# A fused attention and feed-forward block: pacing feed-forward and output matmuls over each query chunk, and filling the free PSUM bank

## The chip, the cores and the metric

The kernel runs on one core of one Trainium2 chip. A core has a matrix engine (PE, TensorE), a vector engine (DVE), an activation engine (ACT), a general engine (POOL), a queue for transfers (SP) and 16 DMA engines. The metric is the device time of one execution in microseconds; the number given for a kernel is the median of several runs.

## The reference

One transformer block on 2048 tokens of width 512, bf16, with attention and feed-forward in parallel, both on the same normalised input:

```
xn  = layernorm(x)                                  # x: 1 x 2048 x 512
qkv = xn @ wqkv                                     # 32 heads of 16
p   = softmax(q @ k.T * 16**-0.5);  A = (p @ v) @ wo
B   = (silu(xn @ w1) * (xn @ w3)) @ w2              # hidden width 1792
out = x + A + B
```

## The kernel before

**Stages.** The head loads x, normalises it, and transposes it into `xnT` (512 x 2048, four blocks of 128 rows). Then attention runs over units: four query chunks of 512 tokens (`NQC`), in each eight groups of four heads (`NG`), in each two halves of 256 queries (the very last half is cut into two of 128). There are 65 units.

Each unit goes through the scores twice. Pass one (`p1`, L755) computes scores with queries on the partitions; each step is two matmuls of 512 keys into a pair of PSUM banks (0 and 1, or 2 and 3), and DVE takes the row maximum of the 128 x 1024 result (L774). 16 steps make a unit of 256 queries, 1024 the whole kernel (`NP1`), 256 a query chunk. The negated maxima are written into spare rows of the query operand, so that pass two (`p2`, L869), which computes the scores again with keys on the partitions, has the maximum already subtracted; ACT takes the exponential out of banks 4 to 6 into one of 44 slots of `PT` (L885, 2048 of them, two for each maximum). The third step, PV, multiplies the exponentials by V (`Vaug`, with a column of ones for the sum of the row) in 16 groups, in bank 7; ACT copies the result out (L949), and two DMAs, a power and a product on POOL normalise it into `onorm`.

Bank 7 is shared, one tenant at a time, by all work that is tiled over columns: the projections QT, KT and V, PV, and the two parts that the change is about. Feed-forward (`ffn_pair`, 14 pairs `G`, `U` for each query chunk, each of four groups of four 512-column matmuls) ends with three ACT evacuations (tanh L627, gate L629, up L633) and three products on POOL into `hT`. The output (`OUT`, four tiles of 128 tokens for each chunk, each one group for x, 14 for `hT` and `w2`, 8 for `onorm` and `wo`) is evacuated by ACT (L688) and stored. For the last chunk the output is in two parts: `OUTA` (x and `hT`, 15 groups a tile, in bank 7, kept in SBUF) and `OUTB` (`onorm`, 8 groups a tile, in banks 0 to 3 once all maxima are taken), added by DVE (L713).

All column-tiled groups are issued by one helper (`col_groups`), so that their matmuls stand under one line, L447. Such a group is four matmuls at once, each into another quarter of the columns of the PE array. `p1` and `p2` are tiled over rows instead: each matmul uses 32 of the 128 rows.

**What sets the order.** The program's order is fixed when it is built. A planner keeps a model of each engine's time with fixed costs (`_c_mm`, `_c_act`, `_c_dve`), and step by step lets the engine go on whose next item could start first. `assign` gives bank 7 to the tile that `choose` names: projections that are due soon, then a PV that is ready, then `outs`, then `ffn` in its order. `pred_g` says when a feed-forward pair may start: its weights have landed, the pair two before it is done, and the output tiles of the chunk before are done (they read `hT`). So before the change the feed-forward of a chunk starts as soon as it may, and runs as fast as bank 7 and its evacuations go. `pick_pe` then decides between a `p1` step (a), a `p2` step (b) and the next column group (c): c goes when it ends before a could start, else a goes, and a b that could start earlier than a goes first.

Semaphores follow from recorded reads and writes. A column group that takes bank 7 waits for the ACT evacuation of the tenant before; PE issues in order, so what is queued behind it waits too.

Of the kernel before, what the change touches and what calls it, by code (L numbers as in the profile page):

```python
# [197 lines left out]


class _Tile:  # L200
    __slots__ = ("groups", "evac", "name", "bank", "pred", "need", "on_start")

    def __init__(self, name, groups, evac, pred=None, need=None, on_start=None):
        self.name = name
        self.groups = groups
        self.evac = evac
        self.pred = pred
        self.need = need
        self.on_start = on_start
        self.bank = None  # L210
# [10 lines left out]
def _c_mm(n):  # L221
    return n / 2400.0 + 0.006


def _build(nc, A_x, A_wqkv, A_wo, B_w1, B_w3, B_w2, out):
    S, D = A_x.shape[1], A_x.shape[2]
    H = D // 16
    NG = H // 4
    DC = D // 128
    F = B_w1.shape[1]  # L230
    FC = F // 128
    NT = S // 128
    NQC = S // 512
# [6 lines left out]
    TOL = 0.15  # L240
    STARVE = 0.7
    COUP = 0.1

    units = []
    for qc in range(NQC):
# [14 lines left out]
    with ctx:  # L260
# [337 lines left out]
            return _Tile("QT2_%d" % u, groups, evac, need=-1)  # L598


        def ffn_pair(sc, fc):
            idx = sc * FC + fc
            sl = idx % 3
            ss = idx % 2
            cnt = [0]

            def part_done(op):
                cnt[0] += 1
                if cnt[0] < 3:
                    return  # L610
                q = poolq["ffn"]
                q.append(_Item(lambda e: e.tensor_scalar(t1[:, :], th[:, ss, :], 1.0, 1.0, ALU.mult, ALU.add),  # L612
                               [("th", ss)], [("t1",)], 0.62, 0.72))
# [12 lines left out]
            def evac_g(bk):  # L626
                return [_Item(lambda e: e.activation(th[:, ss, :], bank(bk), ACTF.Tanh, scale=0.5),  # L627
                              [("ps", bk)], [("th", ss)], _c_act(512), cb=part_done),
                        _Item(lambda e: e.activation(zg[:, ss, :], bank(bk), ACTF.Identity, scale=0.5),  # L629
                              [("ps", bk)], [("zg", ss)], _c_act(512), cb=part_done)]  # L630

            def evac_u(bk):
                return [_Item(lambda e: e.activation(ub[:, ss, :], bank(bk), ACTF.Identity),  # L633
                              [("ps", bk)], [("ub", ss)], _c_act(512), cb=part_done)]

            def pred_g():
                if ("w13", idx) not in done:
                    return False
                if idx >= 2 and ("hT", idx - 2) not in done:
                    return False  # L640
                if sc == 0:
# [6 lines left out]
            return [_Tile("G%d_%d" % (sc, fc), groups(0), evac_g, pred=pred_g, on_start=start_g),  # L648
                    _Tile("U%d_%d" % (sc, fc), groups(1), evac_u)]


        def load_xr(tg):
# [24 lines left out]
        def tile_OUT(tg):  # L677
            qc, ts = divmod(tg, 4)
            groups = [g_x(tg)] + [g_h(ts, fc) for fc in range(FC)]
            groups += [g_on(qc, ts, g, False, g == NG - 1) for g in range(NG)]  # L680

            def evac(bk):
                def cb(op):
                    store(tg)
                    done.add(("OUT", tg))
                    if tg + 4 < NT:
                        load_xr(tg + 4)
                return [_Item(lambda e: e.activation(osb[:, tg % 4, :], bank(bk), ACTF.Identity),  # L688
                              [("ps", bk)], [("osb", tg % 4)], _c_act(512), cb=cb)]
            return _Tile("OUT%d" % tg, groups, evac, pred=lambda: ("xr", tg) in done  # L690
                         and (tg < 4 or ("ST", tg - 4) in done)
                         and all(("hT", qc * FC + fc) in done for fc in range(FC))
                         and all(("ON", qc, g, ts) in done for g in range(NG)))

        def tile_OUTA(tg):
            qc, ts = divmod(tg, 4)
# [28 lines left out]
            p1 += p1_list(u)  # L725
        NP1 = len(p1)
        p1_n = [0]
        red_n = [0]
        pend_fin = []

        def p1_cand():
# [19 lines left out]
            def emit():  # L751
                def f(e):
                    for i in range(2):
                        j = 2 * pair + i
                        ins = e.matmul(bank(2 * sl + i), QT[32 * j:32 * j + 32, qs, q * 128:(q + 1) * 128],  # L755
                                       KT[32 * j:32 * j + 32, g, kc * 512:(kc + 1) * 512],
                                       start=True, stop=True, tile_position=(32 * j, 0))
                    return ins
                P.pe(f, reads, writes, "row", rows, _c_mm(512), name="p1_%d" % n, first="dve")
                p1_n[0] += 1  # L760
                par = u % 2
# [12 lines left out]
                redq.append(_Item(lambda e: e.tensor_reduce(  # L774
                    part[:, par, qt, 2 * pair:2 * pair + 2, kc],
                    ps[:, sl * 1024:(sl + 1) * 1024].rearrange("p (a b) -> p a b", b=512), AX.X, ALU.max),
                    writes, [("part", par, qt, pair, kc)], _c_dve(1024), cb=cb))
# [56 lines left out]
        def p2_cand():  # L834
# [28 lines left out]
            def emit():  # L863
# [3 lines left out]
                def f(e):  # L867
# [4 lines left out]
                                       start=True, stop=True, tile_position=(32 * j, 0))  # L872
                    return ins
                P.pe(f, reads, writes, "row", (j,), kpb * _c_mm(nq), name="p2_%d" % n, first="act")
                p2_n[0] += 1
                pt_slot[(u, kb, j)] = sl
                if not rest:
# [209 lines left out]
        def col_cand():  # L1087
            best = None
            for t in active:
                if not t.groups:  # L1090
                    continue
                g = t.groups[0]
                if g[3] is not None and not g[3]():
                    continue
                reads = g[1]() if callable(g[1]) else g[1]
# [8 lines left out]
            def emit():  # L1104
                g = t.groups.pop(0)
                P.pe(g[0](t.bank), reads, writes, "col", None, dur, name=t.name)
                if len(g) > 4:
                    g[4]()
                if not t.groups:
# [15 lines left out]
            return st, emit, dur  # L1125

        couple = [-1.0]

        def pick_pe():
            a = p1_cand()  # L1130
            b = p2_cand()
            c = col_cand()
            now = P.free["pe"]
            end = max(now, max(P.rg))

# [110 lines left out]
        assert not (expq or miscq or redq or dveq or spq or active or crit or outs or ffn or tail_outs), "stuck"  # L1246
        assert p1_n[0] == NP1 and p2_u[0] == NU and pv_u[0] == NU and all(("ST", t) in done for t in range(NT))

        P.check()
        sems = {e: ctx.enter_context(nc.semaphore("c_" + e)) for e in _ENGS if e != "sp"}  # L1250
        dma_sems = [ctx.enter_context(nc.semaphore("d%d" % i)) for i in range(_NDMA_SEMS)]
# [62 lines left out]
```

## Time and profile before

| | |
|---|---|
| median of 3 runs | 1380.99 us (1380.11 to 1382.21) |
| span of the profiled execution | 1371.5 us |
| PE busy | 1228.5 us (90%) |
| DVE busy | 1215.0 us (89%), of it the row maxima (L774) 1190.2 |
| ACT busy | 1227.7 us (90%), of it the exps (L885) 1095.5 |
| POOL busy | 357.4 us (26%) |
| first and last row maximum start | 19.7 and 1293.6 us |
| first and last exp start | 62.7 and 1364.8 us |

The profile is one execution as the hardware profiler took it; the span is from its first to its last instruction. "Busy" is the time in which an engine has at least one instruction under way; a matmul that is streaming slowly counts as busy as one that is streaming fast. PEclk, beside it, is the share of the full TensorE clock that was granted. A row of a table by stage has the stretch, its length, the busy time with the number of instructions in brackets, then the granted clock, the DMA share and GB/s. A row of the waits has who waited, for whom, the total in us, how often, and the longest.

### The profile page before, as it was taken

How to read it: one execution, taken by the hardware profiler on the slowest of the kernel's cores; microseconds unless marked ns; L12 is line 12 of the kernel's file. 1: busy time of each engine (PE TensorE's matmuls, PEld its weight loads, DVE VectorE, ACT ScalarE, POOL GpSimd, SP SyncE). 2: the span in 40 equal slices, each digit the busy share in tenths (PEclk: the TensorE clock that was granted, in tenths of full speed). 3: DMA queues.
4: the chain of work that ended last, by engine and by line, in shares of the span. 5: the costliest groups of instructions: out<-in, count | busy, mean ns of one | idle time of the engine just before them, and what ended most of it. 6: DMA issues, size and time to landing. Idle time of an engine off the chain costs nothing.

```text
span 1371.5 us, 36041 instructions
## 1 busy us (share of the span) xinstructions
PE 1228.5 (90%) x15257; PEld 435.0 (32%) x15257; DVE 1215.0 (89%) x1141; ACT 1227.7 (90%) x2413; POOL 357.4 (26%) x453
## 2 busy tenths in 40 slices
PE   5988888899999888899999888899999988899998
PEld 2323322333332332333333322333333333233324
DVE  6898999998898999998899999989989999899702
ACT  5698999998898999988899999989989999899864
POOL 4033332211111245411111244421111144431100
PEclk9998999886578999976679999966669999899555
DMA  8011111000000112100000111100001111100000
GB/s 215 5 31 27 25 24 24 18 10 7 9 18 23 40 32 45 33 10 10 8 14 21 39 39 41 39 9 8 10 6 26 33 41 31 38 9 11 5 3 18
DMA packets 112834, 36.07 MB, mean 26 GB/s; under 512 B 98232, under 2 KB 112672, under 8 KB 112672
## 3 DMA queue, kind: packets, MB, share of 16 engines
q1 hardware_dynamic: 112672, 33.76, 11.6%
q8 instruction: 120, 1.97, 0.6%
q14 instruction: 42, 0.34, 0.1%
HBM read 22.81 MB, written 2.10 MB: 18 GB/s over the span
## 4 chain that ended last, share of the span: by engine, by line
PE 58%; ACT 38%; issue 2%; DMA 1%; DVE 0%; SPq 0%; POOL 0%
ACT PT L885 28%; PE ps L447 27%; PE ps L869 20%; PE ps L755 10%; ACT th L627 2%; ACT ub L633 2%; ACT zg L629 2%; ACT QT L573 1%; ACT U L949 1%; ACT KT L530 1%; DMA hT<-in_A_wqkv_dram 1%; ACT osb L688 0%; ACT osb L485 0%; DVE R L938 0%; SPq L380 0%
## 5 line engine op out<-in xcount | busy, mean ns | idle before, releaser
L774 DVE TENSOR_REDUCE part<-ps 128x2 f32<-128x1024 f32 x1024 | 1190.2, 1219 | 83.5 <-PE ps L869 49.1
L885 ACT ACTIVATE PT<-ps 128x512 bf16<-128x512 f32 x2048 | 1095.5, 641 | 109.0 <-PE ps L869 96.6
L869 PE MATMUL ps<-QT,KT 32*128 32x256 bf16 (+1 forms) x4160 | 676.2, 308 | 39.3 <-ACT PT L885 23.8
L755 PE MATMUL ps<-KT,QT 32*128 32x512 bf16 x2048 | 517.9, 434 | 4.3 <-DVE part L774 4.2
L869 PEld LDWEIGHTS ps<-QT,KT 32*128 32x128 bf16 x4160 | 197.9, 96 | 395.0 <-ACT PT L885 314.3
L447 PE MATMUL ps<-PT,Vaug 128*17 128x256 bf16 (+1 forms) x4160 | 214.2, 323 | 14.9 <-ACT ub L633 5.0
L972 POOL TENSOR_TENSOR Rc<-Lc,mone 128x8 f32<-128x8 f32 x62 | 101.4, 1636 | 398.0 <-DMA Lc<-U 397.9
L447 PE MATMUL ps<-xnT,w 128*32 128x512 bf16 x1792 | 144.9, 394 | 45.8 <-ACT zg L629 19.9
L755 PEld LDWEIGHTS ps<-KT,QT 32*128 32x128 bf16 x2048 | 126.0, 95 | 149.3 <-issue 89.8
L447 PEld LDWEIGHTS ps<-PT,Vaug 128*17 128x17 bf16 x4160 | 91.2, 99 | 132.5 <-issue 84.1
L614 POOL TENSOR_TENSOR a<-zg,ub 128x512 f32<-128x512 bf16 x56 | 64.7, 1155 | 128.8 <-ACT ub L633 128.8
L447 PEld LDWEIGHTS ps<-xnT,w 128*32 128x32 bf16 x1792 | 38.5, 95 | 115.8 <-issue 99.8
L616 POOL TENSOR_TENSOR hT<-a,t 128x512 bf16<-128x512 f32 x56 | 71.0, 1268 | 3.2
L791 POOL TENSOR_SCALAR Z<-negm 128x8 bf16<-128x8 f32 x64 | 14.6, 228 | 210.0 <-DVE negm L815 210.0
L447 PE MATMUL ps<-w,hT 128*32 128x512 bf16 x896 | 67.0, 395 | 0.0
L938 DVE RECIPROCAL R<-ps 128x128 f32<-128x128 f32 (+1 forms) x3 | 3.7, 1224 | 63.7 <-PE ps L447 63.7
L994 POOL TENSOR_TENSOR on_b<-U,R 128x256 bf16<-128x256 f32 x32 | 23.2, 725 | 105.8 <-DMA R<-Rrow 105.8
L447 PE MATMUL ps<-xnT,wq 128*32 128x512 bf16 (+2 forms) x576 | 43.4, 388 | 7.8 <-ACT U L949 2.1
L447 PE MATMUL ps<-xnT,wk_on 128*32 128x512 bf16 x512 | 41.7, 402 | 7.9 <-ACT KT L530 4.8
L994 POOL TENSOR_TENSOR wk_on<-U,R 128x256 bf16<-128x256 f32 x30 | 21.8, 727 | 89.3 <-DMA R<-Rrow 89.3
L612 POOL TENSOR_SCALAR t<-th 128x512 f32<-128x512 bf16 x56 | 34.7, 619 | 24.9 <-ACT th L627 22.8
L633 ACT ACTIVATE ub<-ps 128x512 bf16<-128x512 f32 x56 | 34.8, 622 | 1.2 <-PE ps L447 1.2
(73 smaller groups left out, 408.8 us busy)
## 6 DMA issues: line engine op xcount, KB each, us to landing
w<-in_B_w_dram SPq DMA_DIRECT2D x112, 128.0 KB
R<-Rrow SPq DMA_DIRECT2D x248, 16.0 KB
PT<-in_A_x_dram SPq DMA_DIRECT2D x4, 512.0 KB
xr<-in_A_x_dram SPq DMA_DIRECT2D x16, 128.0 KB
out_dram<-osb SPq DMA_DIRECT2D x16, 128.0 KB
QT<-Zs SPq DMA_DIRECT2D x122, 2.0 KB
w<-in_B_w_dram SPq DMA_DIRECT2D x1, 1792.0 KB
hT<-in_A_wqkv_dram SPq DMA_DIRECT2D x3, 512.0 KB
```

Of the source, the lines that this page charges most:

```text
L447: ins = e.matmul(bank(bk)[32 * i:32 * i + m, c0:c0 + ncols], make_lhsT(i), rhs_ap(i), start=start, stop=stop, tile_position=(0, 32 * i), **kw)
L612: q.append(_Item(lambda e: e.tensor_scalar(t1[:, :], th[:, ss, :], 1.0, 1.0, ALU.mult, ALU.add), [("th", ss)], [("t1",)], 0.62, 0.72))
L614: q.append(_Item(lambda e: e.tensor_tensor(a32[:, :], zg[:, ss, :], ub[:, ss, :], ALU.mult), [("zg", ss), ("ub", ss)], [("a32",)], 1.1, 1.25))
L616: q.append(_Item(lambda e: e.tensor_tensor(hT[:, fc, :], a32[:, :], t1[:, :], ALU.mult), [("a32",), ("t1",)], [("hT", fc)], 1.25, 1.35, cb ...
L627: return [_Item(lambda e: e.activation(th[:, ss, :], bank(bk), ACTF.Tanh, scale=0.5), [("ps", bk)], [("th", ss)], _c_act(512), cb=part_don ...
L633: return [_Item(lambda e: e.activation(ub[:, ss, :], bank(bk), ACTF.Identity), [("ps", bk)], [("ub", ss)], _c_act(512), cb=part_done)]
L755: ins = e.matmul(bank(2 * sl + i), QT[32 * j:32 * j + 32, qs, q * 128:(q + 1) * 128], KT[32 * j:32 * j + 32, g, kc * 512:(kc + 1) * 512], ...
L774: redq.append(_Item(lambda e: e.tensor_reduce(part[:, par, qt, 2 * pair:2 * pair + 2, kc], ps[:, sl * 1024:(sl + 1) * 1024].rearrange("p ( ...
L869: ins = e.matmul(bank(b)[:, i * nq:(i + 1) * nq], KT[32 * j:32 * j + 32, g, (k0 + i) * 128:(k0 + i + 1) * 128], QT[32 * j:32 * j + 32, qs, ...
L885: expq.append(_Item(lambda e: e.activation(PT[:, sl, :], bank(b), ACTF.Exp, scale=SCALE), [("ps", b)], [("PT", sl)], _c_act(512), cb=cb))
L972: poolq["nrm"].append(_Item(lambda e: e.tensor_tensor(Rc[:, pp, 0:nl], Lc[:, pp, 0:nl], mone[:, 0:nl], ALU.pow), [("Lc", pp), ("mone",)], ...
L994: poolq["nrm"].append(_Item(lambda e: e.tensor_tensor(onorm[ob][:, g, q0:q0 + nq], U[:, us, 0:nq], R[:, pp, 0:nq], ALU.mult), [("U", us)] ...
```

## The change

There are two edits, both in the planner; no engine gets another kind of instruction.

*Pacing.* The counter `p1_n` of issued `p1` steps serves as a clock. A feed-forward pair `fc` of chunk `sc` may not start before `ffn_from(sc, fc)`: the 14 starts are spread evenly from count 40 to 300 in chunk 0, from 100 after the chunk's start to 44 after its end in chunks 1 and 2, and from 868 to 1000 in the last. Besides, each group of a `G`, `U` or `OUT` tile needs a positive balance of tokens: a `p1` step adds 3000 (up to 4096 in all), a group takes 2048, the columns that its four matmuls stream. `OUTA`, `OUTB`, PV and the projections are not paced. After the last `p1` step no group is.

*Filling.* Each matmul step is logged with the time at which the planner starts it and with its columns (1024 for `p1`, 512 for `p2`, 1024 for a PV group, 2048 for another column group). When there is no column group to issue, bank 7 has no tenant, `p1_n` is at least 64 and under 1024, and the log of the last 3.0 us holds fewer than 11200 columns, a spare group goes into bank 7: four matmuls of 512 columns with `ident` as weights and `xnT` as data. Nothing reads what it writes.

```
--- before.py
+++ after.py
@@ -198,10 +198,11 @@
 
 
 class _Tile:
-    __slots__ = ("groups", "evac", "name", "bank", "pred", "need", "on_start")
-
-    def __init__(self, name, groups, evac, pred=None, need=None, on_start=None):
+    __slots__ = ("groups", "evac", "name", "bank", "pred", "need", "on_start", "paced")
+
+    def __init__(self, name, groups, evac, pred=None, need=None, on_start=None, paced=False):
         self.name = name
+        self.paced = paced
         self.groups = groups
         self.evac = evac
         self.pred = pred
@@ -240,6 +241,11 @@
     TOL = 0.15
     STARVE = 0.7
     COUP = 0.1
+    PACE = 3000
+    PACE_CAP = 4096
+    LAG = 44
+    LOAD_WIN = 3.0
+    LOAD_MIN = 11200
 
     units = []
     for qc in range(NQC):
@@ -598,6 +604,14 @@
             return _Tile("QT2_%d" % u, groups, evac, need=-1)
 
 
+        CHUNK = 2 * NG * 16
+
+        def ffn_from(sc, fc):
+            last = sc == NQC - 1
+            lo = sc * CHUNK + (100 if sc else 40)
+            hi = (sc + 1) * CHUNK + (-24 if last else LAG)
+            return lo + (hi - lo) * fc // FC
+
         def ffn_pair(sc, fc):
             idx = sc * FC + fc
             sl = idx % 3
@@ -638,6 +652,8 @@
                     return False
                 if idx >= 2 and ("hT", idx - 2) not in done:
                     return False
+                if p1_n[0] < ffn_from(sc, fc):
+                    return False
                 if sc == 0:
                     return all(("V", t) in done for t in range(NT)) and not _wk_pending() and not _wq_pending()
                 return all(("OUT", (sc - 1) * 4 + ts) in done for ts in range(4))
@@ -645,8 +661,8 @@
             def start_g():
                 if idx + 2 < NQC * FC:
                     load_w13(idx + 2)
-            return [_Tile("G%d_%d" % (sc, fc), groups(0), evac_g, pred=pred_g, on_start=start_g),
-                    _Tile("U%d_%d" % (sc, fc), groups(1), evac_u)]
+            return [_Tile("G%d_%d" % (sc, fc), groups(0), evac_g, pred=pred_g, on_start=start_g, paced=True),
+                    _Tile("U%d_%d" % (sc, fc), groups(1), evac_u, paced=True)]
 
 
         def load_xr(tg):
@@ -690,7 +706,7 @@
             return _Tile("OUT%d" % tg, groups, evac, pred=lambda: ("xr", tg) in done
                          and (tg < 4 or ("ST", tg - 4) in done)
                          and all(("hT", qc * FC + fc) in done for fc in range(FC))
-                         and all(("ON", qc, g, ts) in done for g in range(NG)))
+                         and all(("ON", qc, g, ts) in done for g in range(NG)), paced=True)
 
         def tile_OUTA(tg):
             qc, ts = divmod(tg, 4)
@@ -725,6 +741,7 @@
             p1 += p1_list(u)
         NP1 = len(p1)
         p1_n = [0]
+        tokens = [0]
         red_n = [0]
         pend_fin = []
 
@@ -758,6 +775,8 @@
                     return ins
                 P.pe(f, reads, writes, "row", rows, _c_mm(512), name="p1_%d" % n, first="dve")
                 p1_n[0] += 1
+                tokens[0] = min(tokens[0] + PACE, PACE_CAP)
+                note_load(st, 1024)
                 par = u % 2
 
                 def cb(op):
@@ -872,6 +891,7 @@
                                        start=True, stop=True, tile_position=(32 * j, 0))
                     return ins
                 P.pe(f, reads, writes, "row", (j,), kpb * _c_mm(nq), name="p2_%d" % n, first="act")
+                note_load(st, 512)
                 p2_n[0] += 1
                 pt_slot[(u, kb, j)] = sl
                 if not rest:
@@ -1092,6 +1112,8 @@
                 g = t.groups[0]
                 if g[3] is not None and not g[3]():
                     continue
+                if t.paced and tokens[0] <= 0 and p1_n[0] < NP1:
+                    continue
                 reads = g[1]() if callable(g[1]) else g[1]
                 writes = [("ps", t.bank)]
                 st = P.pe_start("col", None, P.ready("pe", reads, writes))
@@ -1104,6 +1126,9 @@
             def emit():
                 g = t.groups.pop(0)
                 P.pe(g[0](t.bank), reads, writes, "col", None, dur, name=t.name)
+                if t.paced:
+                    tokens[0] -= 2048
+                note_load(st, 1024 if t.name.startswith("PV") else 2048)
                 if len(g) > 4:
                     g[4]()
                 if not t.groups:
@@ -1125,11 +1150,33 @@
             return st, emit, dur
 
         couple = [-1.0]
+        loadlog = []
+
+        def note_load(st, w):
+            loadlog.append((st, w))
+            while loadlog and loadlog[0][0] < st - LOAD_WIN:
+                loadlog.pop(0)
+
+        def fill_cand():
+            if 7 in bank_tenant or head_tiles or p1_n[0] < 64 or p1_n[0] >= NP1:
+                return None
+            writes = [("ps", 7)]
+            st = P.pe_start("col", None, P.ready("pe", (), writes))
+            if sum(w for t, w in loadlog if t >= st - LOAD_WIN) >= LOAD_MIN:
+                return None
+
+            def emit():
+                P.pe(col_groups(7, lambda i: ident[:, 32 * i:32 * i + 32], lambda i: xnT[:, 0, 0:512], 512),
+                     [("ident",)] + xnT_keys(0, 512), writes, "col", None, _c_mm(512), name="fill")
+                note_load(st, 2048)
+                n_fill[0] += 1
+            return st, emit, _c_mm(512)
+        n_fill = [0]
 
         def pick_pe():
             a = p1_cand()
             b = p2_cand()
-            c = col_cand()
+            c = col_cand() or fill_cand()
             now = P.free["pe"]
             end = max(now, max(P.rg))
 
@@ -1246,6 +1293,7 @@
         assert not (expq or miscq or redq or dveq or spq or active or crit or outs or ffn or tail_outs), "stuck"
         assert p1_n[0] == NP1 and p2_u[0] == NU and pv_u[0] == NU and all(("ST", t) in done for t in range(NT))
 
+        P.n_fill = n_fill[0]
         P.check()
         sems = {e: ctx.enter_context(nc.semaphore("c_" + e)) for e in _ENGS if e != "sp"}
         dma_sems = [ctx.enter_context(nc.semaphore("d%d" % i)) for i in range(_NDMA_SEMS)]
```

More of the change, by code (lines that the diff above doesn't have):

```diff
@@ L200, with __init__ @@
 class _Tile:
-    __slots__ = ("groups", "evac", "name", "bank", "pred", "need", "on_start")
-    def __init__(self, name, groups, evac, pred=None, need=None, on_start=None):
+    __slots__ = ("groups", "evac", "name", "bank", "pred", "need", "on_start", "paced")
+    def __init__(self, name, groups, evac, pred=None, need=None, on_start=None, paced=False):
         self.name = name
+        self.paced = paced
         self.groups = groups
@@ L242, in _build @@
     COUP = 0.1
+    PACE = 3000
+    PACE_CAP = 4096
+    LAG = 44
+    LOAD_WIN = 3.0
+    LOAD_MIN = 11200
     units = []
@@ L598, in tile_QT2, with ffn_from @@
             return _Tile("QT2_%d" % u, groups, evac, need=-1)
+        CHUNK = 2 * NG * 16
+        def ffn_from(sc, fc):
+            last = sc == NQC - 1
+            lo = sc * CHUNK + (100 if sc else 40)
+            hi = (sc + 1) * CHUNK + (-24 if last else LAG)
+            return lo + (hi - lo) * fc // FC
         def ffn_pair(sc, fc):
@@ L640, in pred_g @@
                     return False
+                if p1_n[0] < ffn_from(sc, fc):
+                    return False
                 if sc == 0:
@@ L647, in start_g @@
                     load_w13(idx + 2)
-            return [_Tile("G%d_%d" % (sc, fc), groups(0), evac_g, pred=pred_g, on_start=start_g),
-                    _Tile("U%d_%d" % (sc, fc), groups(1), evac_u)]
+            return [_Tile("G%d_%d" % (sc, fc), groups(0), evac_g, pred=pred_g, on_start=start_g, paced=True),
+                    _Tile("U%d_%d" % (sc, fc), groups(1), evac_u, paced=True)]
         def load_xr(tg):
@@ L692, in tile_OUT @@
                          and all(("hT", qc * FC + fc) in done for fc in range(FC))
-                         and all(("ON", qc, g, ts) in done for g in range(NG)))
+                         and all(("ON", qc, g, ts) in done for g in range(NG)), paced=True)
         def tile_OUTA(tg):
@@ L727, in _build @@
         p1_n = [0]
+        tokens = [0]
         red_n = [0]
@@ L760, in emit @@
                 p1_n[0] += 1
+                tokens[0] = min(tokens[0] + PACE, PACE_CAP)
+                note_load(st, 1024)
                 par = u % 2
@@ L874, in emit @@
                 P.pe(f, reads, writes, "row", (j,), kpb * _c_mm(nq), name="p2_%d" % n, first="act")
+                note_load(st, 512)
                 p2_n[0] += 1
@@ L1094, in col_cand @@
                     continue
+                if t.paced and tokens[0] <= 0 and p1_n[0] < NP1:
+                    continue
                 reads = g[1]() if callable(g[1]) else g[1]
@@ L1106, in emit @@
                 P.pe(g[0](t.bank), reads, writes, "col", None, dur, name=t.name)
+                if t.paced:
+                    tokens[0] -= 2048
+                note_load(st, 1024 if t.name.startswith("PV") else 2048)
                 if len(g) > 4:
@@ L1127, in _build, with note_load, fill_cand, emit @@
         couple = [-1.0]
+        loadlog = []
+        def note_load(st, w):
+            loadlog.append((st, w))
+            while loadlog and loadlog[0][0] < st - LOAD_WIN:
+                loadlog.pop(0)
+        def fill_cand():
+            if 7 in bank_tenant or head_tiles or p1_n[0] < 64 or p1_n[0] >= NP1:
+                return None
+            writes = [("ps", 7)]
+            st = P.pe_start("col", None, P.ready("pe", (), writes))
+            if sum(w for t, w in loadlog if t >= st - LOAD_WIN) >= LOAD_MIN:
+                return None
+            def emit():
+                P.pe(col_groups(7, lambda i: ident[:, 32 * i:32 * i + 32], lambda i: xnT[:, 0, 0:512], 512),
+                     [("ident",)] + xnT_keys(0, 512), writes, "col", None, _c_mm(512), name="fill")
+                note_load(st, 2048)
+                n_fill[0] += 1
+            return st, emit, _c_mm(512)
+        n_fill = [0]
         def pick_pe():
@@ L1131, in pick_pe @@
             b = p2_cand()
-            c = col_cand()
+            c = col_cand() or fill_cand()
             now = P.free["pe"]
@@ L1247, in _build @@
         assert p1_n[0] == NP1 and p2_u[0] == NU and pv_u[0] == NU and all(("ST", t) in done for t in range(NT))
+        P.n_fill = n_fill[0]
         P.check()
```

## The prediction

> **What bounds the kernel now.** I read the page first: the span, the engines' shares, the slices.
>
> ```profile
> span 1371.5 us, 36041 instructions
> PE 1228.5 (90%) x15257; PEld 435.0 (32%) x15257; DVE 1215.0 (89%) x1141; ACT 1227.7 (90%) x2413; POOL 357.4 (26%) x453
> DVE  6898999998898999998899999989989999899702
> PEclk9998999886578999976679999966669999899555
> ```
>
> Three engines stand at about 90%, so none is an obvious bound. The last row tells more: the granted TensorE clock sinks four times, and where it sinks DVE's digit goes from 9 to 8. The medians before are at 1380.99 us and the span is 1371.5, so 9.5 us lie around the span; I add them at the end. With runs from 1380.11 to 1382.21, about 0.2% (2.8 us) is what can be told from no change.
>
> Next the waits, for what DVE (the row maxima, L774) and ACT (the exps, L885) stand still for.
>
> ```profile
> ACT PT L885 <- PE ps L869: 96.6, 183, 2.8
> DVE part L774 <- PE ps L869: 49.1, 91, 1.3
> DVE part L774 <- PE ps L755: 25.2, 31, 4.9
> ```
>
> Both wait for score matmuls on PE, DVE for 74.3 us in all. That is the store from which a faster PE could pay while maxima run.
>
> Then the row maxima (L774) by stage. The columns are from:to, length, DVE busy (count), granted clock, DMA. The last row is from a narrower stretch; an instruction on a border is counted on both sides, so I take one off each count.
>
> ```profile
> 265.00:435.00 170.00, 152.27 (x131) 0.70 0.06 12
> 435.00:590.00 155.00, 151.67 (x132) 0.98 0.17 36
> 590.00:710.00 120.00, 106.08 (x91) 0.67 0.05 8
> 780.00:900.00 120.00, 115.91 (x101) 0.97 0.17 35
> 900.00:1025.00 125.00, 110.74 (x95) 0.63 0.05 9
> 1260.00:1295.00 35.00, 32.36 (x28) 0.69 0.05 7
> 1295.00:1371.50 76.50, 0.00 (x0) 0.54 0.03 10
> 1203.00:1260.00 57.00, 56.26 (x50) 1.00 0.05 9
> ```
>
> The four low-clock stretches (0.63 to 0.70) are 450 us with 345 - 4 = 341 maxima: 1.320 us each. The three full-clock stretches (0.97 to 1.00) are 332 us with 283 - 3 = 280: 1.186 us each. In the latter DVE is busy 97 to 99% of the time, so DVE is the bound there; in the low-clock ones (88 to 92%) PE is. The last 76.5 us have no maximum at all: a tail of exps, second matmuls and output. So the kernel is bound by DVE at full clock, by PE at the low clock, and by PE again in the tail.
>
> What makes the clock sink? I cut the trace at the borders at which it changes, 3.41 us apart. First two steps of all PE work, then the column-tiled matmuls (the helper's L447) of the second of them.
>
> ```profile
> 341.36:344.77 3.41, 3.41 (x22) 0.50 0.13 19
> 395.96:399.37 3.41, 3.41 (x62) 1.00 0.06 7
> 395.96:399.37 3.41, 2.59 (x44) 1.00 0.06 7
> ```
>
> Both steps have PE busy from end to end; one is granted 0.50, the other 1.00. So it is not busy time that decides; the steps differ in how many matmuls stream, 22 against 62. Now one step that is followed by a fall and one that is followed by a rise: for each its L447 matmuls, how many of these are PV (the tile view of PT), its L755, its L869, and the clock of the step after.
>
> ```profile
> 402.79:406.20 3.41, 0.51 (x12) 1.00 0.02 5
> 402.79:406.20 3.41, 1.39 (x6) 1.00 0.02 5
> 402.79:406.20 3.41, 1.92 (x14) 1.00 0.02 5
> 406.20:409.61 3.41, 3.41 (x50) 0.50 0.09 19
> 433.51:436.92 3.41, 2.21 (x20) 0.50 0.04 7
> 433.51:436.92 3.41, 0.00 (x0) 0.50 0.04 7
> 433.51:436.92 3.41, 1.40 (x4) 0.50 0.04 7
> 433.51:436.92 3.41, 1.23 (x10) 0.50 0.04 7
> 436.92:440.33 3.41, 3.41 (x62) 1.00 0.10 15
> ```
>
> (In the first step the tile view gives the same row as L447: all 12 are PV, of 256 columns.) Columns streamed: 12 x 256 + 6 x 512 + 14 x 256 = 9,700, and the clock falls; 20 x 512 + 4 x 512 + 10 x 256 = 14,800, and it rises. The switching point lies between, if columns are the measure. The change's own mark, 11200 in 3.0 us, is 12,700 in 3.41: inside.
>
> The Trainium skill ("TensorE: Matmul & The Clock Gate", "What's actually happening" and "HAM oscillation") has a clock of half or full by windows of about 3.4 us, which the trace shows, and says that PE keeps it as long as no idle gap exceeds about 3.4 us. The trace differs on that: the step at 341.36 was busy for all of its 3.41 us at 0.50. By that rule neither spreading nor fills would matter to the clock.
>
> **The change part by part.** *Spreading.* It removes no matmul of the reference. Columns per maximum follow from the counts of the groups:
>
> ```profile
> L869 PE MATMUL ps<-QT,KT 32*128 32x256 bf16 (+1 forms) x4160 | 676.2, 308 | 39.3 <-ACT PT L885 23.8
> L755 PE MATMUL ps<-KT,QT 32*128 32x512 bf16 x2048 | 517.9, 434 | 4.3 <-DVE part L774 4.2
> L447 PE MATMUL ps<-PT,Vaug 128*17 128x256 bf16 (+1 forms) x4160 | 214.2, 323 | 14.9 <-ACT ub L633 5.0
> L447 PE MATMUL ps<-xnT,w 128*32 128x512 bf16 x1792 | 144.9, 394 | 45.8 <-ACT zg L629 19.9
> L447 PE MATMUL ps<-w,hT 128*32 128x512 bf16 x896 | 67.0, 395 | 0.0
> L447 PE MATMUL ps<-xnT,wq 128*32 128x512 bf16 (+2 forms) x576 | 43.4, 388 | 7.8 <-ACT U L949 2.1
> ```
>
> Over 1024 maxima: scores for the exps 4160 x 256 / 1024 = 1,040, for the maxima 1,024, PV 1,040, Q at most 288: 3,390, in a 3.41 us step (2.9 maxima at 1.18) 9,800. That is the load of the low-clock stretches, under the mark. Feed-forward adds 896 per maximum, 2,600 per step: 12,400 when spread evenly, about at the mark. Today it runs at twice that in half of the time. While OUT runs (x896 and the rest of its groups), its pace is capped by the tokens at 3000 columns per maximum, 8,700 per step, well above the mark. So spreading alone makes every step marginal, and the fill must carry the rest.
>
> *The fill.* It needs bank 7 empty and under 11200 columns in the last 3 us. A fill is four matmuls into four column groups: by the step at 395.96, 44 L447 matmuls or 11 groups in 3.41 us beside full maxima and exps, it takes 0.31 us of PE. Short of the mark by a few hundred to 2,900 columns a step, one group of 2,048 in one step of two or three is enough: I estimate 100 to 150 fills, 30 to 45 us of PE. That lies beside DVE's maxima, which stand at 97 to 99% with more column groups than that in the full-clock stretches; if that cover were gone it would be the 30 to 45 us. Each fill also waits for the ACT evacuation that empties bank 7, and maxima and exp matmuls queue behind it on PE. The nearest row:
>
> ```profile
> PE ps L447 <- ACT zg L629: 24.3, 35, 1.2
> ```
>
> 0.7 us each time. Bounds: 0 (the planner puts the fill after the evacuation) to 100 x 0.7 = 70; I take 4 us, since such waits stand now in full-clock stretches that still run at 1.186.
>
> *Sum while maxima run.* The four low-clock stretches at the full-clock pace: 341 x (1.320 - 1.186) = 46 us gained. Less dense feed-forward leaves ACT fewer evacuations to crowd into the full-clock stretches: at best the pace of 1203:1260, 57 / 49 = 1.163, for the other 667 maxima, 15 us; I take 5. Against: steps in which bank 7 is held by a PV that waits for exps cannot be filled; a sixth of the 46, 8 us. With 4 for the waits: 46 + 5 - 8 - 4 = 39.
>
> *The tail.* Exps (L885) at full clock before the tail and in it, then a step of the tail: all PE, and its L447.
>
> ```profile
> 1203.00:1260.00 57.00, 52.00 (x98) 1.00 0.05 9
> 1295.00:1371.50 76.50, 40.89 (x71) 0.54 0.03 10
> 1303.91:1307.32 3.41, 3.41 (x22) 0.50 0.00 0
> 1303.91:1307.32 3.41, 2.02 (x16) 0.50 0.00 0
> ```
>
> 71 exps take 76.5 us, 1.08 each; at full clock it is 57 / 97 = 0.59. In the tail PE is busy throughout, and alternates a column group of OUTB with an exp's matmuls: 4 groups in 3.41 us, 8,192 + 6 x 256 = 9,700 columns, which keeps the clock low, while the same order at full clock would stream almost twice that and keep it high. The tail's first steps thus depend on the clock with which it begins, and the fills hold it until the last maximum is issued. Bounds: 71 x (1.08 - 0.59) = 35 gained, or nothing. Also, OUTA (4 x 15 = 60 groups, unpaced) now comes after a last pair that starts at count 868 + 132 x 13 / 14 = 991 or later, so 33 maxima or 39 us before the end. It needs 60 x 0.31 = 19 us of PE; a last pair and two PVs share bank 7 with it. I put one tile of four into the tail, 15 x 0.31 = 5 us. I take 20 - 5 = 15 us gained.
>
> Sum: 1371.5 - 39 - 15 = 1317.5, with 9.5 around it 1327.
>
> **The rivals.** *A: the even load sits under the switching point everywhere (slower).* For it: 12,400 is only at the mark, and the planner's microseconds are shorter than the chip's. Against: the fill. The 667 other maxima would then also go at 1.320: 667 x 0.134 = 89 us, 1470. It decides if the mean granted clock while maxima run is under about 0.8.
>
> *B: the tail takes it back.* All of OUTA spills and the clock is low from the start: 60 groups at 3.41 / 4 = 0.85 us are 51 us. With 39 gained it is 12 slower (1393); with half of OUTA, 14 faster, 1367. For it: feed-forward ends where the maxima end. Against: dense OUTA groups are what raises the clock.
>
> *C: columns are not the measure, and the fill does nothing for the clock.* The clock then sinks for as much of the time as now: nothing gained, 4 us for the fill's waits, 1381 to 1385. For it: the two steps differ in more than columns. By the Trainium skill's rule on idle gaps, above, it would come out so. Against: the pair of flips above.
>
> **How the numbers follow.** My forecast has 0.76, A 0.06, B 0.13, C 0.05. The forecast's own bounds: best 46 + 15 in the maxima, 27 in the tail, so 88 less, 1293; worst half of the 39 and 4 in the tail, 1357. The range 1296 to 1358 leaves out A, C and B's worse half. Slower: A, B's worst third, half of C: 0.12 is 0.06 + 0.04 + 0.02; same: the rest of C, 0.03; faster 0.85.
>
> **What would show it.** Right: PEclk 9 throughout up to the tail; 1.17 to 1.20 us per maximum in every stage; DVE's wait for PE well under 74.3 us; feed-forward tanh (L627) in nearly every slice; 100 to 150 groups of four with ident and xnT as operands; last maximum near 1255; a tail of about 62 us with a clock over 0.54. Wrong: a clock under 0.9 while maxima run (A or C), OUTA groups beside OUTB in a tail over 76 us (B), or ACT's exps falling further behind the maxima than the 71 that are left in the tail now.

## The result, and the profile after

The changed kernel took 1348.56 us (median of 4 runs, 1331.87 to 1371.74) against 1380.98 before (1380.11 to 1382.21): a ratio of 0.9734, 95% interval 0.9669 to 0.9798. A second comparison of the same two programs (e1 below) gave 1352.63 (1331.41 to 1355.98) against 1380.72: 0.9711 (0.9618 to 0.9803). Runs more than 1.5% above the shortest of their program (1371.74 here, 1355.49 and 1355.98 in e1) are left out of these ratios, which is why they are lower than the quotients of the medians, 0.977 and 0.980. By the ratios it is faster by 2.7 to 2.9%; by the medians it is some 30 us, where 54 were forecast (1327 us, range 1296 to 1358).

The program's own runs spread over 40 us, and the mean granted clock goes with them: 1331.9 at 0.935, 1349.4 at 0.915, 1355.5 at 0.905, 1371.7 at 0.888, about 8.5 us for each 0.01. The one execution profiled with the result was the longest of all, 1371.7; the profile shown here is that of e1, the same program at 1355.5 us.

Lines moved with the edit: L793 is now the row maximum (L774 before), L905 the exp (L885), L772 and L888 the score matmuls of the two passes (L755, L869), L453 the column groups (L447), L641 the tanh. First its page.

```profile
span 1353.5 us, 37002 instructions
PE 1236.3 (91%) x15793; PEld 436.6 (32%) x15793; DVE 1211.9 (90%) x1141; ACT 1221.9 (90%) x2413; POOL 357.7 (26%) x453
DVE  6899999899889998897999999999989999899911
PEclk8979989799869998885989999998989999798996
L453 PE MATMUL ps<-xnT,ident 128*32 128x512 bf16 x536 | 53.8, 443 | 1.7 <-ACT QT L579 1.2 <-ACT U L969 0.4
```

The four broad valleys of the clock are gone; in their place are many shallow ones, spread over the whole span. There are 536 / 4 = 134 fills. The waits and the stages, in the same cuts as before:

```profile
ACT PT L905 <- PE ps L888: 67.5, 132, 1.7
DVE part L793 <- PE ps L888: 37.0, 69, 1.0
DVE part L793 <- PE ps L772: 36.1, 46, 5.0
```

```profile
265.00:435.00 170.00, 156.95 (x135) 0.87 0.10 20
435.00:590.00 155.00, 147.68 (x130) 0.92 0.12 25
590.00:710.00 120.00, 104.35 (x89) 0.76 0.12 23
780.00:900.00 120.00, 117.00 (x102) 0.97 0.14 28
900.00:1025.00 125.00, 118.30 (x103) 0.93 0.13 25
1287.00:1353.50 66.50, 1.08 (x1) 0.85 0.04 11
```

In this execution DVE waits for PE as long as before (73.1 us against 74.3). The old valleys take 4 and 8 maxima more in the first and last of these cuts, but in 590:710 two fewer, at a higher clock (0.76 against 0.67); and the old peak of 435:590 loses two. The last maximum starts at 1286.9 us instead of 1293.6: 6.7 us. The tail after it is 66.6 us instead of 77.9: 11.3 us. Together they are the 18.0 us by which this execution's span is shorter than the profiled one of before. That is a little over half of the 32.4 us between the medians: the profiled execution of before took about 1373.5 us (its span and 2 us around it, see below), 7.5 under its median, and this one is 6.9 over 1348.56. No execution of the changed program near 1331 us was profiled.

### The profile page after: what moved, and what is told of

Read it like the earlier page. It is cut to its first block, busy times and chain, and to the rows that moved or that the text cites. A ratio compares the mean times of both kernels' runs of the same rounds, so it can differ in the third digit from the quotient of the medians.

```text
span 1369.9 us, 37002 instructions
## 1 busy us (share of the span) xinstructions
PE 1253.8 (92%) x15793; PEld 440.0 (32%) x15793; DVE 1213.3 (89%) x1141; ACT 1223.3 (89%) x2413; POOL 358.5 (26%) x453
## 4 chain that ended last, share of the span: by engine, by line
PE 48%; ACT 43%; DVE 4%; issue 2%; DMA 1%; SPq 1%; POOL 0%
ACT PT L905 34%; PE ps L453 26%; PE ps L888 14%; PE ps L772 8%; DVE part L793 4%; ACT th L641 2%; ACT ub L647 2%; ACT zg L643 2%; ACT U L969 1%; ACT QT L579 1%; ACT KT L536 1%; DMA hT<-in_A_wqkv_dram 1%; ACT osb L704 0%; ACT osb L491 0%; DVE R L958 0%
## 5 line engine op out<-in xcount | busy, mean ns | idle before, releaser
L793 DVE TENSOR_REDUCE part<-ps 128x2 f32<-128x1024 f32 x1024 | 1189.1, 1218 | 94.8 <-PE ps L888 46.1
L905 ACT ACTIVATE PT<-ps 128x512 bf16<-128x512 f32 x2048 | 1088.4, 623 | 98.5 <-PE ps L888 83.7
L888 PE MATMUL ps<-QT,KT 32*128 32x256 bf16 (+1 forms) x4160 | 633.3, 293 | 31.3 <-ACT PT L905 20.5
L772 PE MATMUL ps<-KT,QT 32*128 32x512 bf16 x2048 | 490.5, 420 | 7.0 <-DVE part L793 6.1
L888 PEld LDWEIGHTS ps<-QT,KT 32*128 32x128 bf16 x4160 | 197.2, 95 | 394.2 <-ACT PT L905 324.4
L453 PE MATMUL ps<-PT,Vaug 128*17 128x256 bf16 (+1 forms) x4160 | 194.6, 306 | 11.9 <-ACT osb L704 3.4
L453 PE MATMUL ps<-xnT,w 128*32 128x512 bf16 x1792 | 163.6, 429 | 28.9 <-ACT zg L643 9.8
L772 PEld LDWEIGHTS ps<-KT,QT 32*128 32x128 bf16 x2048 | 122.1, 94 | 139.6 <-issue 75.4
L453 PEld LDWEIGHTS ps<-PT,Vaug 128*17 128x17 bf16 x4160 | 89.7, 97 | 109.8 <-issue 63.3
L453 PE MATMUL ps<-w,hT 128*32 128x512 bf16 x896 | 79.0, 402 | 0.0
L453 PEld LDWEIGHTS ps<-xnT,w 128*32 128x32 bf16 x1792 | 33.4, 96 | 106.1 <-issue 94.5
L453 PE MATMUL ps<-xnT,ident 128*32 128x512 bf16 x536 | 54.9, 453 | 1.6 <-ACT QT L579 1.2
L453 PE MATMUL ps<-xnT,wk_on 128*32 128x512 bf16 x512 | 45.2, 425 | 5.2 <-ACT KT L536 2.4
L453 PE MATMUL ps<-xnT,wq 128*32 128x512 bf16 (+2 forms) x576 | 43.4, 381 | 6.6 <-ACT ub L647 3.4
```

Source lines behind the costliest of these rows:

```text
L453: ins = e.matmul(bank(bk)[32 * i:32 * i + m, c0:c0 + ncols], make_lhsT(i), rhs_ap(i), start=start, stop=stop, tile_position=(0, 32 * i), **kw)
L793: redq.append(_Item(lambda e: e.tensor_reduce(part[:, par, qt, 2 * pair:2 * pair + 2, kc], ps[:, sl * 1024:(sl + 1) * 1024].rearrange("p ( ...
L888: ins = e.matmul(bank(b)[:, i * nq:(i + 1) * nq], KT[32 * j:32 * j + 32, g, (k0 + i) * 128:(k0 + i + 1) * 128], QT[32 * j:32 * j + 32, qs, ...
L905: expq.append(_Item(lambda e: e.activation(PT[:, sl, :], bank(b), ACTF.Exp, scale=SCALE), [("ps", b)], [("PT", sl)], _c_act(512), cb=cb))
```

## The experiments

Theory T: the clock is granted step by step, 3.41 us each, by what PE streams, with a switch; the change gains by the steps that it lifts over it. Rivals: S, the gain comes from spreading ACT's and DVE's work; C, the clock answers to PE's busy time or gaps, not to columns. All edits are against the changed kernel.

**e1, no edit.** 

> The changed kernel again, unaltered, to see how far its own runs spread. Theory T (the clock is granted by the columns streamed in each 3.41 us step, with a switch at about 12,300, and the planned 11200 in 3.0 us comes out at just that on the chip): the same program lands between about 1330 and 1372 us from run to run, and the time follows the mean granted clock, about 8 us less for each 0.01. Theory S (the gain comes from spreading the ACT and DVE work; the clock is a bystander): time does not follow the clock.

1331.41 at 0.935, 1349.77 at 0.913, 1355.49 at 0.905, 1355.98 at 0.904: the time follows the clock, as T has it. Counted over e1's trace (columns of all matmuls that start in each step, each matmul by its width, 512, 256 or 128): of steps at full clock followed by another, 95% had 12,288 or more; of those followed by half, the middle one had 11,900; of steps at half followed by half, 95% had 12,000 or fewer; of those followed by full, the middle one had 12,700. Steps with 11,000 to 13,500 are found on both sides when a matmul counts whole in the step in which it starts. When its columns are shared out over the steps that it lies in (its end is modelled), the two sorts hardly overlap: a single mark of 12,000 columns tells the clock of the next step rightly in 5,191 of the 5,268 steps from 60 us on in all fourteen traces (the two kernels and e1 to e12; the fills of e6 counted as four quarters). So there is a switch, near 12,000 to 12,300 columns, which the two steps of the prediction had only put between 9,700 and 14,800.

**e2, pacing alone.**

```
-    LOAD_MIN = 11200
+    LOAD_MIN = 0
```

> Pacing alone, no fills (LOAD_MIN = 0). T: even feed-forward carries 12,400 columns a step, output more, and everything between them 9,800, so the clock drops in more places than before, mean clock about 0.75 to 0.85, time 1375 to 1430 us. S: all of the gain stays, 1335 to 1350. Clock-by-busy-time (C): as the changed kernel, since PE is no less busy.

1380.7 us against 1380.72: 1.0014 (0.9981 to 1.0048). No gain: S falls. The mean clock is higher than before (0.845 to 0.867 against 0.834 to 0.848) and it buys nothing in sum. From its page DVE and the clock, then the row maxima's view of its tail (a run of 1391 us):

```profile
span 1389.5 us, 35897 instructions
DVE  5889899898799999998889999989888989998932
PEclk9979699787578997996779899977677989896999
1330.50:1389.50 59.00, 1.06 (x1) 0.97 0.05 12
```

DVE's digits are at 8 in more places than before. The last maximum comes later (1330.3 us), but the tail is 59 us at clock 0.97, not 78 at 0.54: output groups that pacing pushed into it (140 matmuls that read `hT`) stream there. So the clock rises in the tail and sinks while maxima run (from 60 us to the last, 0.84 against 0.86 before).

**e3, fills alone.**

```
-        self.paced = paced
+        self.paced = False
...
-                if p1_n[0] < ffn_from(sc, fc):
-                    return False
```

> Fills alone: feed-forward and output run as soon as they may, as before, and the spare group is issued under the same mark. T: the stretches without feed-forward, which stood at 0.63 to 0.70, are filled to the mark and come up to about 0.9; mean clock 0.90 or more, time 1320 to 1350, as the changed kernel or better. S: no gain, 1375 to 1390. C: as before, 1381, plus up to 5 for the fills.

1347.41 us (1346.47 to 1364.58): 0.9789 (0.9722 to 0.9857), an interval that overlaps that of both together (0.9669 to 0.9798). 211 fills in place of 134. So fills carry the change, and pacing adds nothing that can be told apart from zero.

**e4, a higher mark.**

```
-    LOAD_MIN = 11200
+    LOAD_MIN = 13500
```

> Pacing and fills with the mark raised from 11200 to 13500 columns in 3.0 us (15,400 in 3.41 us). T: well above the switch even where the chip is some per cent behind the plan, so fewer steps at half clock, mean clock 0.94 or more, time 1300 to 1335 and less spread. S: slower than the changed kernel by the added fills (some 40 groups of 0.31 us at most, 12 us). C: the same.

1329.78 us (1326.12 to 1337.59): 0.9638 (0.9581 to 0.9694), clock 0.932 to 0.946. The old valleys in its profile, row maxima:

```profile
265.00:435.00 170.00, 167.32 (x146) 0.99 0.10 19
590.00:710.00 120.00, 111.95 (x98) 0.89 0.11 21
900.00:1025.00 125.00, 116.97 (x102) 0.89 0.10 21
```

170 / 145 = 1.172 us a maximum in the first: the pace of a full clock, where before it was 1.31. The mark of 11200 was too near the switch: 12,700 columns in 3.41 us of the planner's time, and the chip is slower than the plan (an exp is 0.479 us in the plan; in the prediction's stretch at full clock 97 exps keep ACT busy for 52.00 us, 0.54 each).

**e5, fills of a quarter of the columns.**

```
-... ident[:, 32 * i:32 * i + 32], lambda i: xnT[:, 0, 0:512], 512),
+... ident[:, 32 * i:32 * i + 32], lambda i: xnT[:, 0, 0:128], 128),
```

> The changed kernel with its 134 fills at the same places in the order, but each of their four matmuls streams 128 columns and not 512. Theory T (columns streamed set the clock): as pacing alone, mean clock 0.85 to 0.87, time 1373 to 1392. Rival C (an instruction in the gap, the mode switch or PE's busy time sets it): as the changed kernel, clock about 0.91, 1331 to 1372 with a middle near 1350.

1393.1 us: 1.0091 (1.0062 to 1.012), clock 0.841 to 0.858. C falls: the same 134 insertions at the same places do nothing for the clock. The median is 12.4 us over that of e2, but this is not the price of the insertions: without fills the planner makes another order. Of the two profiled executions, the last maximum starts at 1332.0 us here and at 1330.3 in e2, 1.7 us later; the tail is 67.8 us and not 59.2, and there no fill stands.

**e6, fills over the whole array.** One matmul with 128 columns of weights in place of four with 32.

```
-                P.pe(col_groups(7, lambda i: ident[:, 32 * i:32 * i + 32], lambda i: xnT[:, 0, 0:512], 512),
+                P.pe(lambda e: e.matmul(bank(7), ident[:, :], xnT[:, 0, 0:512], start=True, stop=True),
```

> The changed kernel with the same fills, each one matmul of 512 columns over the whole array (128 rows by 128 columns of weights) in place of four that use a quarter each. It takes the array as long. T1 (what counts is columns times matmuls): a fill counts 512 and not 2048, so as pacing alone, clock 0.85 to 0.87, 1373 to 1392 us. T2 (what counts is the share of the array that works): a fill counts as much as before, clock about 0.91, middle near 1350.

1362.51 us (1356.55 to 1366.72): 0.9852 (0.9797 to 0.9906), clock 0.894 to 0.908. That is the changed kernel's band of clocks (0.888 to 0.935), though in its lower half, and far from e2's (0.845 to 0.867). So such a matmul counts about as much as four quarters: what is counted looks like the share of the array that works, T2, and T1 falls. The steps of its trace say the same: with columns shared out as under e1, the best mark tells the clock of the next step in 357 of 378 steps if a fill counts as one quarter, in 369 if as three and in 372 if as four. Whether it counts exactly as much stays open; the ratio's interval touches that of the changed kernel only at its edge. The fills of the two experiments, for the time that they take on PE:

```profile
L453 PE MATMUL ps<-xnT,ident 128*32 128x128 bf16 x536 | 27.6, 249 | 1.6 <-ACT QT L579 1.2 <-ACT U L969 0.4
L1169 PE MATMUL ps<-xnT,ident 128*128 128x512 bf16 x134 | 52.3, 440 | 1.8 <-ACT QT L579 1.2 <-ACT U L969 0.4
```

The 134 fills are 52.3 us busy over the whole array, and 53.8 as sets of four quarters (e1): the same time for about the same effect on the clock.

**e7, a still higher mark.** `LOAD_MIN = 16000`.

> Pacing and fills with the mark at 16000 columns in 3.0 us. If the clock has a switch at about 12,300 a step and 13500 is already clear of it, more fills buy nothing where bank 7 is free: clock 0.94 to 0.95 as with 13500, and PE's extra groups may cost DVE a little, 1325 to 1340 us. If the clock answers smoothly to the load, clock 0.96 and 1310 to 1320.

1370.86 us (1349.94 to 1390.79), clock 0.880 to 0.924: neither. Its profile (a run of 1355.15 us) has the earlier maxima at the pace of e4 (855 from 100 to 1110 us, against 849), and loses from about count 912 on, where the last chunk's feed-forward is paced most densely, and in the tail after it (87.1 us against 70.7). The row maxima from there and the column groups of a step, then the row maxima from the same time to the last in e4:

```profile
1111.00:1266.00 155.00, 131.28 (x112) 0.72 0.12 26
1172.41:1175.82 3.41, 1.47 (x12) 0.50 0.28 54
```

```profile
1111.00:1259.00 148.00, 136.29 (x117) 0.87 0.13 27
```

That is 155 / 111 = 1.40 us a maximum here and 148 / 116 = 1.28 in e4. In that step three feed-forward groups stream, 6,144 columns; with the scores it has some 10,000. A feed-forward tile holds bank 7 while ACT evacuates it, so no fill can go, whatever the mark.

**e8, fills alone with the mark at 13500.** The edits of e3 and e4.

> Fills alone with the mark at 13500, without pacing. T: the stretches without feed-forward come to full clock wherever bank 7 is free, the dense stretches stand there already, clock about 0.93, 1325 to 1340 us: then pacing brings nothing once the fill has its margin. If pacing matters by itself (fewer steps in which bank 7 is held and idle), 10 to 20 us slower than pacing with the same mark.

1330.72 us (1326.11 to 1343.16): 0.9639 (0.9574 to 0.9704), the same as e4. With a margin on the mark, too, pacing brings nothing in sum.

**e9, fills in the tail as well.** e8, and

```
-            if 7 in bank_tenant or head_tiles or p1_n[0] < 64 or p1_n[0] >= NP1:
+            if 7 in bank_tenant or head_tiles or p1_n[0] < 64 or p2_u[0] >= NU:
```

> Fills alone with the mark at 13500, and allowed until the last unit's second scores are issued, not only until the last maximum. In the run that stops at the last maximum the tail after it took about 79 us, most of it at half clock. Theory T: with the tail at full clock for most of its length it takes about 60, so 1310 to 1322 us against 1331. Rival: in the tail PE itself is the bound and a fill takes what it gives, 1328 to 1340.

1331.65 us: 0.966 (0.9615 to 0.9705), no different from e8. The exps in the tails of e8 and of e9:

```profile
1260.50:1341.40 80.90, 55.77 (x99) 0.67 0.04 10
```

```profile
1258.30:1337.50 79.20, 58.20 (x99) 0.82 0.04 10
```

With 24 more fills in it the tail's clock is 0.82 and not 0.67, and it is 1.7 us shorter. T's 15 to 20 us fail; the outcome is the rival's, that a fill in the tail takes about what it gives.

**e10 and e11, the last chunk unpaced.** e4, with pacing for `G` and `U` only where `sc < NQC - 1`; e10 has the tail edit of e9 besides, e11 not.

```
-                if p1_n[0] < ffn_from(sc, fc):
+                if sc < NQC - 1 and p1_n[0] < ffn_from(sc, fc):
...
-            return [_Tile("G%d_%d" % (sc, fc), groups(0), evac_g, pred=pred_g, on_start=start_g, paced=True),
-                    _Tile("U%d_%d" % (sc, fc), groups(1), evac_u, paced=True)]
+            return [_Tile("G%d_%d" % (sc, fc), groups(0), evac_g, pred=pred_g, on_start=start_g, paced=sc < NQC - 1),
+                    _Tile("U%d_%d" % (sc, fc), groups(1), evac_u, paced=sc < NQC - 1)]
```

> Pacing and fills with the mark at 13500, the last chunk's feed-forward not paced, and fills allowed in the tail. T: the half-clock steps of the last chunk (counts 912 to 1023, where paced feed-forward holds bank 7 and streams 11,000 to 12,300 columns a step) go, and the tail stays at full clock: 1300 to 1318 us, clock 0.95 or more. Rival: these steps only move elsewhere, 1325 to 1335.

> The same without fills in the tail: pacing and fills with the mark at 13500, the last chunk's feed-forward not paced. T: counts 912 to 1023 about 8 us shorter than with pacing there, but output groups no longer fall into the tail and the clock there drops, up to 15 us longer; 1320 to 1338 in sum. Against the run with fills in the tail the difference is the tail alone, 10 to 20 us.

The tail edit found no place for a fill here, so PE's order is the same in both: eight runs of one program. e10: 1322.83 us (1320.89 to 1324.84), 0.9588 (0.9554 to 0.9621); e11: 1324.5 (1323.64 to 1341.96), 0.9635 (0.957 to 0.9699). What the tail's fills do in this version was therefore not tried. With e12 this is the shortest version found, some 25 us under the changed kernel. It lies between T's 1300 to 1318 us and the rival's 1325 to 1335, and by the intervals it can't be told apart from e4. Against what was expected of e11, output groups still fall into the tail (108 matmuls that read `hT`). Its page (e10), the row maxima's last stretch and the exps of its tail:

```profile
span 1323.0 us, 37549 instructions
DVE  5899999999999998899899999999999999899902
PEclk8979999999999997898699999899999999799997
1110.00:1252.00 142.00, 136.17 (x118) 0.94 0.14 29
1252.20:1323.00 70.80, 50.52 (x86) 0.88 0.05 11
```

DVE is at 9 nearly everywhere while maxima run. The tail has 86 exps left, not 71: ACT falls further behind the maxima than before.

**e12, the same with the mark at 16000.** e11 and `LOAD_MIN = 16000`.

> The best version so far (pacing and fills, the last chunk's feed-forward not paced) with the mark at 16000 in place of 13500. With pacing everywhere, 16000 took 1350 to 1391 us against 1326 to 1338, and its profile stands at a low clock from count 912 on, where the last chunk's paced feed-forward holds bank 7. If that place is the cause, it is gone here: 1315 to 1328 us, as with 13500. If too many fills are themselves the cost (PE too full for the maxima), 1345 or more.

1324.28 us (1318.8 to 1338.26): 0.9643 (0.9565 to 0.972). So the loss of e7 is the last chunk's pacing; 254 fills by themselves do no harm. The stretch from about count 912 on, at 134 / 107 = 1.25 us a maximum and not 1.40:

```profile
1111.00:1245.00 134.00, 124.81 (x108) 0.89 0.13 27
```

## Why the prediction was right in direction and too large

**The mechanism holds.** That the clock sinks where too little of the array streams, that the fills lift it, that spreading alone would not (e2: 1.0014), and that there would be 100 to 150 fills (134) was so. The switch lies at about 12,000 to 12,300 columns a step, between the two steps on which the argument stood. Of rival C nothing is left (e5). A did not come to pass: from 60 us to the last maximum the clock is 0.91 in e1 and 0.89 in the longest run, not under 0.8. Other signs that the prediction named for being right did not come: the clock is not at 9 throughout, the old valleys stand at up to 120 / 88 = 1.36 us a maximum and not at 1.17 to 1.20, DVE waits for PE as long as before, and the last maximum is at 1286.9 us and not near 1255.

The Trainium skill ("TensorE: Matmul & The Clock Gate", "What's actually happening") says that the window of the clock gate is free-running and does not begin with the kernel. The traces agree: the first border of the 3.41 us grid comes 0.36 us after the first instruction in e1 and 2.00 us after it in the execution profiled with the result, which is the same program; in e10 and e11, one program too, it is 1.60 and 3.20 us. By that, a program whose steps lie at the switch would be lifted or dropped by where the grid falls, and the spread of one program from 1331 to 1372 us would follow. This consequence is argued, not shown, by two pairs of traces. The eight runs of e10 and e11, at a higher mark, spread over half as much, 1321 to 1342 us.

**The step that failed: "a sixth of the 46, 8 us".** This was the share of half-clock steps that would remain. Counted from 60 us to the last maximum, 66 steps stand at half clock in e1's trace, against 100 before: two thirds remain. And they are not the same kind of steps. Before, an L755 row of a half-clock step with column work and of one without, each followed by its L447 row:

```profile
331.12:334.53 3.41, 2.04 (x4) 0.50 0.00 0
331.12:334.53 3.41, 1.62 (x32) 0.50 0.00 0
341.36:344.77 3.41, 2.09 (x7) 0.50 0.13 19
341.36:344.77 3.41, 0.00 (x0) 0.50 0.13 19
```

With no column group in it, a step at half clock issues the scores of three maxima, as many as at full clock (6 matmuls and one on the border): it costs next to nothing. With column groups in it, two. Of the 100 half-clock steps before, 35 had none; of e1's 66, one. On average the 35 see 2.80 maxima start, the other 65 see 2.08, and steps at full clock 2.93. So the steps that cost were 65 and are 65, which would be why DVE's wait for PE did not shrink and the last maximum comes only 6.7 us sooner. The change turned the nearly free steps into steps at full clock, and left, or made anew, as many of the costly kind. Pacing alone makes them 114 (e2), fills alone leave 62 (e3). A step of e1, in the last chunk (L772, L453, and all PE):

```profile
1167.72:1171.13 3.41, 1.43 (x4) 0.50 0.15 28
1167.72:1171.13 3.41, 1.74 (x16) 0.50 0.15 28
1167.72:1171.13 3.41, 3.41 (x30) 0.50 0.15 28
```

Scores for two maxima, a feed-forward tile, PE full, and bank 7 taken. By the same count e4 has 38 costly steps and e10 has 31. DVE's wait for PE goes with them, in e2 and in e10:

```profile
DVE part L793 <- PE ps L772: 57.0, 84, 5.2
DVE part L793 <- PE ps L888: 54.6, 109, 1.3
DVE part L793 <- PE ps L772: 24.8, 24, 5.2
DVE part L793 <- PE ps L888: 21.4, 42, 1.3
```

So does the start of the last maximum: 1244.8 us with 28 costly steps (e12), 1259.0 with 38 (e4), 1286.9 with 65 (e1), 1330.3 with 114 (e2), about 1 us for each. Reckoned from the maxima, two in place of 2.9, a costly step loses 0.9 x 1.17 = 1.05 us; the 34 that e10 has fewer than before make 36 us, and its last maximum starts at 1252.2, 41 us sooner. In other words the forecast's 39 us while maxima run were there to be had, but not with the mark at 11200; e4, which changes only the mark, reaches 35 of them.

I had priced every maximum of the low-clock stretches alike (1.320 - 1.186) and so missed that the price sits in the steps with column work.

**The tail: 15 forecast, 11.3 measured (e1).** The bounds of 0 to 35 held. But the reason was partly another: "one tile of four" of OUTA was to spill, as a cost of 5 us. In e1 the matmuls that read `hT` after the last maximum are 168 of OUTA's 224, three tiles of four, and the clock is 0.85 there. In e3, which differs only in pacing, none is left for the tail; its clock is 0.65, 93 exps are left and it is 76.9 us long. Rival B's premise came true for three tiles and its sign did not. How much of the 11.3 us the clock brings stays open: in e9 a higher clock in the tail, by fills, is worth 1.7 us.

```profile
1287.00:1353.50 66.50, 15.91 (x168) 0.85 0.04 11
```

**The waits of the fills: 4 us forecast.** PE stood idle for 1.7 us in all just before fills (the L453 row of e1), and in e5 the last maximum starts 1.7 us later than in e2. Neither is the price by itself, but nothing here asks for more than the 4 us. PE's time for the fills, which the sum put at nothing because other work covers it, is 53.8 us, not 30 to 45; no run shows by itself what it costs DVE.

**The 9.5 us "around the span".** They were read wrongly. The profiled runs after the change end 1.8 to 2.0 us above their span (1371.74 for 1369.9, 1355.49 for 1353.5). So the profiled execution of before had taken about 1373.5 us, less than any of the three runs shown; later runs of it go from 1371.9 to 1390.2, so 2.8 us was also too little for what can be told from no change. Of the 9.5 us, 2 lie around the span and 7.5 are how far this execution was under its median. The sum of 54 us holds for this execution and would have put it at 1319.5; that the 7.5 us come on top for the changed kernel is a guess. Smaller: the "other 667 maxima" are 683 (1024 - 341), which changes rival A's 89 us to 92 and not the sum.

**ACT falling behind**, named as a sign of failure, is not one: the run that gains most (e10) has 86 exps left in its tail.

## What to carry to other kernels

Where a kernel's matmuls use part of the array (32 rows, or 17 columns), read the granted clock step by step beside what streams in each step, not beside PE's busy share; and price a low-clock step by what the bounding engine loses in it, since some cost next to nothing. Work that is to hold a clock over a switch needs a margin over the plan's own error (from 11200 to 13500 it was worth some 20 us more), and a place to go when the shared bank is taken. Spreading real work evenly is no substitute: here it was worth 0.0014 of the wrong sign, within its interval of nothing.

## What the runs showed of the hardware that was not expected

- PE can be busy for all of a 3.41 us step and be granted half of the clock (before, 341.36:344.77). The switch is near 12,000 to 12,300 columns of quarter-array matmuls in a step, and a matmul over the whole array counts for about four (e6).
- A low clock can last although PE is full: in e7 from 1111 to 1266 us (0.72), 19 of 25 steps at half clock are followed by another, and in these scores and column groups in turn stream 8,900 to 12,100 columns a step, shared out as under e1, with PE busy for 92% of the step or more.
- One program on one core varied from 1331 to 1372 us, with its mean clock from 0.935 to 0.888; the 3.41 us grid of the clock lay differently against the program in each of its two profiled executions.
